# Seven-product blocks from block 3 on, strided keys first among a batch's loads, squares on either engine, a ring of three for xT, and tiled column sums

## The chip, the cores and the metric

One core of one Trainium2 chip. The time is that of one execution on the device, in microseconds; medians are given with their range. Runs are called slow when they lie more than 1.5% above the fastest of the same kernel, and medians, ranges and ratios here are of the other, fast runs alone. Five engines work side by side: TensorE (PE in the profile; PEld its weight loads), VectorE (DVE), ScalarE (ACT), GpSimd (POOL) and SyncE (SP).

## The reference

Eight batches of attention with eight heads (576 positions, 64 wide), then a feed-forward layer on 4608 tokens. Four heads look at the last 32 positions ("local"), four at every 32nd one ("strided").

```python
scores = scale * np.matmul(q, k.transpose(0, 1, 3, 2))
mask_local = (rel >= 0) & (rel < stride)
mask_strided = (rel >= 0) & (pos[None, :] % stride == pos[:, None] % stride)
# ... masked softmax, times v; heads 0-3 local, 4-7 strided; then x is [4608, 512]
h = x @ w_in                     # 512 -> 2048
r = np.maximum(h, 0.0)
g = s * (r * r) + b
return (g @ w_out).astype(np.float32)
```

Since g = s * r^2 + b, the kernel computes s * (r^2 @ w_out) + b * (column sums of w_out).

## The kernel before

A scheduler within the Python program fixes the order of all instructions before anything runs. It keeps an account of when each engine is free and when each result will be there; a job that several engines can do goes to the one that its account says is done first. In the traces each engine runs its work in that order, so a job whose input is there can still stand behind another job of its engine.

```python
LAT = {"A": 70.0, "V": 70.0, "P": 70.0, "D": 12000.0, "X": 7000.0, "Y": 12000.0}   # ns until a result counts as there
# in flush(), for a job p that is ready at r:
eng = min(p[1], key=lambda e: max(self.free[e], r) + p[1][e])
...
self.done[k] = end + (6000.0 if soon else p[4] or self.LAT[eng])
```

"D" stands for a transposing DMA on SyncE's queue. Loads of a batch, issued by GpSimd, in the order local q, local k, strided q, strided k. They are held back by a real dependency, a gate: GpSimd first reads one element of the transposed strided keys of the batch before.

```python
def fetch_qk(b):
    for mm in range(2):
        if (b - 1, "kTs", mm) in loaded:                    # the gate
            nc.gpsimd.tensor_copy(out=gate[0:1, 2 + mm:3 + mm],
                                  in_=loaded[b - 1, "kTs", mm][0:1, 0, 0:1])
    load_qk(b)
    # ... the account notes when each will have landed
# the issue of a batch's loads costs GpSimd nothing in the account:
plan.post([...], {"P": 0.0}, lambda eng, b=b: fetch_qk(b + 2), [("fetch", b + 2)])
```

From batch 3 on the strided queries are turned by a DMA transpose (qT) and then spread out into a tile with zeros between heads (qD_str), which the scores read. Three engines are offered for the spread:

```python
plan.post([("in", "q" + sfx, b, mm), ("q", (b - 2, m))], {"D": 1300.0}, q_dma, [("qT", id_)])
plan.post([("qT", id_), ("s", (b - 1, m), 2)], {"P": 2000.0, "V": 940.0, "A": 1340.0}, q_spread,
          [("q", id_)])
```

The feed-forward runs in nine blocks of 512 tokens. Its second product is either 64 matmuls of 512 columns, or, from block `SEVEN` on (5 here), seven half-size products of 16 matmuls of 256 columns, with sums made by VectorE. Squares, in the blocks before `SEVEN`, are on VectorE alone:

```python
([("u", T, ft)], {"V": 430, **({"A": 600} if T >= SEVEN else {})}, sq, [("g", T, ft)])
# column sums of w_out, spread over all 128 partitions: 16 of
nc.tensor.matmul(out=gts["b"], lhsT=ones16, rhs=w_out_sb[:, ft, :], start=(ft == 0), stop=(ft == NFT - 1))
```

The softmax here doesn't subtract the row's maximum and nothing guards it: scores larger than these inputs give would overflow.

## Time and profile before

| | before |
|---|---|
| time, first three runs | 311.81 us (311.32 to 312.32) |
| span of the profiled run, mean granted clock | 310.4 us, 0.996 |
| TensorE, VectorE, ScalarE, GpSimd busy | 301.5, 215.6, 182.7, 97.3 us |
| TensorE's excess (see below), of it from 30 us to the last matmul | 9.1 us, 3.1 us |

"Excess" is used throughout. For each matmul in the timeline, it is the distance to the next matmul's start less columns/2.4 + 2.5 ns, what that matmul needs at the full clock. Its sum is TensorE's lost time, whether it waits or runs at a lower clock. The tiled column sums and the FP32 matmul are left out of it and counted by themselves. The prediction below shows and reads the lines.

### The profile page before, as it was taken

How to read it: one execution, taken by the hardware profiler on the slowest of the kernel's cores; microseconds unless marked ns; L12 is line 12 of the kernel's file. 1: busy time of each engine (PE TensorE's matmuls, PEld its weight loads, DVE VectorE, ACT ScalarE, POOL GpSimd, SP SyncE). 2: the span in 40 equal slices, each digit the busy share in tenths (PEclk: the TensorE clock that was granted, in tenths of full speed). 3: DMA queues.
4: the chain of work that ended last, by engine and by line, in shares of the span. 5: the costliest groups of instructions: out<-in, count | busy, mean ns of one | idle time of the engine just before them, and what ended most of it. 6: DMA issues, size and time to landing. Idle time of an engine off the chain costs nothing.

```text
span 310.4 us, 6706 instructions
## 1 busy us (share of the span) xinstructions
PE 301.5 (97%) x2524; PEld 195.2 (63%) x2524; DVE 215.6 (69%) x573; ACT 182.7 (59%) x341; POOL 97.3 (31%) x140
## 2 busy tenths in 40 slices
PE   8898999999999999999999999999999999999994
PEld 3764655666556566556697755465577676767883
DVE  7566758898977788747674775679776467747552
ACT  2776854689846788368265856575945455456200
POOL 8562559921871095029500961000000000000000
PEclk9999999999999999999999999999999999999998
DMA  7999999994999899979999999953010100300313
GB/s 128 188 207 205 215 172 163 214 176 101 92 134 158 128 99 161 142 153 108 162 153 183 131 148 131 159 131 107 2 36 34 68 10 26 105 0 0 105 59 113
DMA packets 99924, 37.28 MB, mean 120 GB/s; under 512 B 81154, under 2 KB 95874, under 8 KB 99890
## 3 DMA queue, kind: packets, MB, share of 16 engines
q0 software_dynamic: 57200, 18.08, 59.1%
q1 hardware_dynamic: 42690, 18.76, 30.8%
q8 instruction: 20, 0.33, 0.4%
q14 instruction: 14, 0.11, 0.1%
HBM read 36.84 MB, written 10.32 MB: 152 GB/s over the span
## 4 chain that ended last, share of the span: by engine, by line
PE 88%; DMA 8%; POOL 1%; ACT 1%; issue 0%; DVE 0%; SPq 0%; POOLq 0%
PE ps_f L862 37%; PE ps_f L911 22%; PE ps_f L833 12%; DMA ql<-in_q_dram 6%; PE ps_s L528 5%; PE ps_a L582 3%; DMA w_out_sb<-in_v_dram 2%; PE ps_s L833 2%; PE ps_t L408 2%; PE ps_a L833 1%; PE ps_t L582 1%; PE ps_a L934 1%; PE ps_t L833 1%; PE ps_t L630 1%; POOL v_loc L312 1%
## 5 line engine op out<-in xcount | busy, mean ns | idle before, releaser
L862 PE MATMUL ps_f<-xT,w_in_sb 128*128 128x512 f16 (+1 forms) x632 | 146.6, 357 | 0.2 <-ACT u L884 0.2
L884 ACT ACTIVATE u<-ps_f 128x512 f16<-128x512 f32 x140 | 82.8, 596 | 74.0 <-PE ps_f L862 71.6
L862 PEld LDWEIGHTS <-w_in_sb 128*128 128x128 f16 x640 | 68.0, 113 | 35.7 <-issue 0.8
L911 PE MATMUL ps_f<-w_out_sb,gT 128*128 128x512 f16 x320 | 85.1, 379 | 0.0
L893 DVE TENSOR_TENSOR gT<-u 128x512 f16<-128x512 f16 x112 | 46.3, 418 | 33.2 <-ACT u L884 32.4
L911 PEld LDWEIGHTS <-gT 128*128 128x128 f16 x320 | 29.2, 98 | 23.6 <-DVE gT L893 0.6
L833 PEld LDWEIGHTS <-gT 128*128 128x128 f16 x320 | 31.0, 98 | 8.4
L833 PE MATMUL ps_f<-w_out_sb,gT 128*128 128x256 f16 x176 | 24.6, 273 | 0.0
L608 DVE TENSOR_TENSOR x_nat<-ps_a,rec 72x256 f16<-72x256 f32 (+1 forms) x52 | 23.8, 457 | 0.5
L544 ACT ACTIVATE p_loc<-ps_s 128x384 f16<-128x384 f32 x46 | 21.0, 494 | 3.4 <-PE ps_s L528 2.7
L544 ACT ACTIVATE p_str<-ps_s 72x432 f16<-72x432 f32 (+1 forms) x46 | 20.8, 482 | 3.2 <-PE ps_s L528 2.9
L290 POOL DMA_DIRECT2D v_loc<-in_v_dram x28 | 20.5, 741 | 2.3 <-DMA kl<-in_k_dram 1.2
L582 PEld LDWEIGHTS <-p_str 72*128 72x128 f16 x256 | 15.2, 98 | 9.5 <-DVE x_nat L608 0.2
L891 ACT ACTIVATE gT<-u 128x512 f16<-128x512 f16 x32 | 19.8, 629 | 0.8
L922 DVE SCALAR_TENSOR_TENSOR o<-ps_f,s_sb,bcs 128x512 f32<-128x512 f32 x20 | 14.9, 747 | 5.6 <-PE ps_f L911 5.1
L966 POOL COPY gate<-kT 1x1 f16<-1x1 f16 x6 | 1.8, 300 | 45.3 <-DMA kT<-ks 45.3
L597 DVE RECIPROCAL rec<-ps_a 72x4 f32<-72x4 f32 (+1 forms) x52 | 9.2, 178 | 9.4 <-PE ps_a L582 8.9
L552 DVE TENSOR_TENSOR p_loc<-p_loc,mask_loc 128x384 f16<-128x384 f16 x42 | 14.0, 349 | 2.5 <-ACT p_loc L544 2.2
L295 POOL DMA_DIRECT2D v_str<-in_v_dram x16 | 13.0, 816 | 8.6 <-DVE rec L597 2.7
L552 DVE TENSOR_TENSOR p_str<-p_str,mask_str 72x432 f16<-72x432 f16 (+1 forms) x42 | 14.3, 353 | 1.0 <-ACT p_str L544 0.7
L833 PEld LDWEIGHTS <-S 128*128 128x128 f16 x128 | 12.5, 98 | 3.9 <-issue 0.8
L582 PEld LDWEIGHTS <-p_loc 128*128 128x128 f16 x192 | 10.5, 98 | 4.8
(152 smaller groups left out, 407.1 us busy)
## 6 DMA issues: line engine op xcount, KB each, us to landing
out_dram<-o SPq DMA_DIRECT2D x35, 256.0 KB, 4.7
w_out_sb<-in_moe_w_out_dram POOLq DMA_DIRECT2D x4, 512.0 KB, 11.4
v_loc<-in_v_dram POOLq DMA_DIRECT2D x28, 72.0 KB, 8.4
ql<-in_q_dram POOLq DMA_DIRECT2D x6, 288.0 KB, 6.6
qs<-in_q_dram POOLq DMA_DIRECT2D x6, 288.0 KB, 6.8
ks<-in_k_dram POOLq DMA_DIRECT2D x6, 288.0 KB, 7.2
kl<-in_k_dram POOLq DMA_DIRECT2D x4, 288.0 KB, 7.9
kl<-in_k_dram POOLq DMA_DIRECT2D x16, 72.0 KB, 3.4
```

The source lines that it names most:

```text
L290: nc.gpsimd.dma_start(out=vl[LPAD:128, h, :, 0:D], in_=v_band(b, h))
L528: nc.tensor.matmul(out=st["s", g][0:nk, c:c + 2 * nq], lhsT=(st["k"][:, i * nq:i * nq + nk] if loc else st["k"][:, i, 0:SQ]), rhs=st["q"][ ...
L544: nc.scalar.activation(out=pt[0:nk, 0:2 * n].rearrange("k t c -> k (t c)"), in_=st["s", g][0:nk, 0:2 * n * nq], func=AF.Exp, scale=scale)
L552: nc.vector.tensor_tensor(out=pt[0:nk, 0:2 * n], in0=pt[0:nk, 0:2 * n], in1=mask, op=ALU.mult)
L582: nc.tensor.matmul(out=st["a"][:, j % per, :], lhsT=st["pw", g][0:nk, i * nq:i * nq + WIDE], rhs=vt[0:nk, 2 * mm + e, j, :])
L608: nc.vector.tensor_tensor(out=st["x"][:, j0:j0 + per, 64 * e:64 * e + 64], in0=st["pa", e, j][0:nq, 0:per, 0:D], in1=st["rec", e, j][0:nq, ...
L833: nc.tensor.matmul(out=gts[name, T][:, t], lhsT=lhs(k, t), rhs=rhs(k), start=fresh and t == k == 0, stop=t == 1 and k == H - 1, skip_group ...
L862: nc.tensor.matmul(out=gts["h", T, ft][:, lo:hi], lhsT=w_in_sb[min(ft // 4, 2)][:, ct].rearrange("p (c x l) -> p c l x", x=128, l=4)[:, ma ...
L884: nc.scalar.activation(out=gts["u", T, ft], in_=gts["h", T, ft], func=AF.Relu)
L891: nc.scalar.activation(out=gts[T][:, ft, :], in_=u, func=AF.Square)
L893: nc.vector.tensor_tensor(out=gts[T][:, ft, :], in0=u, in1=u, op=ALU.mult)
L911: nc.tensor.matmul(out=gts[id_], lhsT=gts[T][:, ft, ts * 128:(ts + 1) * 128], rhs=w_out_sb[:, ft, cols], start=(ft == 0), stop=(ft == NFT ...
```

## The change

Intent: less work for the bound engine (seven products in two more blocks; column sums in a quarter of the array each; a wait less in the last block), and room for it elsewhere (squares on either engine, a smaller ring). Core of the diff:

```diff
-                self.done[k] = end + (6000.0 if soon else p[4] or self.LAT[eng])
+                self.done[k] = end + (6000.0 if soon else p[4] or
+                                           (5500.0 if eng == "D" and end < 110000.0 else self.LAT[eng]))
-    NX = 4
+    NX = 3
+    KS_FIRST = 3
     def load_qk(b):
+        if b >= KS_FIRST:
+            load_qs("k", k)          # strided keys before the local q and k
         for name, src in (("q", q), ("k", k)):
             ...                      # local
+        load_qs("q", q)
+        if b < KS_FIRST:
+            load_qs("k", k)
-    SEVEN = 5
+    SEVEN = 3
-  ([("u", T, ft)], {"V": 430, **({"A": 600} if T >= SEVEN else {})}, sq, [("g", T, ft)])
+  ([("u", T, ft)], {"V": 430, **({"A": 630})}, sq, [("g", T, ft)])
-    def bcs_step(ft, group):         # 16 matmuls of 128 x 512
+    def bcs_steps(group):
+                for c in chunks:
+                    for g in range(4):
+                        nc.tensor.matmul(
+                            out=gts["b"][32 * g:32 * g + 32], lhsT=ones16[:, 0:32],
+                            rhs=w_out_sb[:, 4 * c + g, :], start=(c == 0), stop=(c == 3), ...)
+        # ScalarE copies the partial sums out; one FP32 matmul by 1/32 adds the four groups
+            nc.tensor.matmul(out=gts["b"], lhsT=part32, rhs=gts["b_sb"], start=True, stop=True)
 # (cut: the last block's product W in two PSUM banks, its stores in halves; the account's arrival
 #  times follow the new order of loads; positions of block 0's steps)
```

More of the change, by code (lines that the diff above doesn't have):

```diff
@@ L179 @@
     ones16 = w_mix[4].rearrange("p f m -> p (f m)")[:, 0:128]
+    part32 = w_mix[4].rearrange("p f m -> p (f m)").bitcast(FP32)[:, 64:192]
     w_mix[1] = w_out_sb[:, 0:NFT // 2, DM // 2:DM]
@@ L241 @@
     nc.vector.memset(ones16, 1.0)
+    nc.vector.memset(part32, 1.0 / 32)
     nc.vector.memset(vl_stage[0:LPAD], 0.0)
@@ L257, with load_qs @@
     paired = {}
+    KS_FIRST = 3
     def load_qk(b):
+        def load_qs(name, src):
+            if name == "k":
+                ts = ks[b % 2]
+            elif b < QS_DMA + 2:
+                ts = inp.tile([SR, NS], FP16, tag="qs", name="qs")
+            else:
+                ts = loaded[b - 2, "qs"]
+            if name == "k" and b in (2, 3) or name == "q" and b in (QS_DMA, QS_DMA + 1):
+                nc.gpsimd.memset(ts[64:SR], 0.0)
+            load_s(ts, src, b)
+            loaded[b, name + "s"] = ts
+        if b >= KS_FIRST:
+            load_qs("k", k)
         for name, src in (("q", q), ("k", k)):
@@ L270, in load_qk @@
                 nc.gpsimd.dma_start(out=h4(tl), in_=view_l(src, b))
-        for name, src in (("q", q), ("k", k)):
-            if name == "k":
-                ts = ks[b % 2]
-            elif b < QS_DMA + 2:
-                ts = inp.tile([SR, NS], FP16, tag="qs", name="qs")
-            else:
-                ts = loaded[b - 2, "qs"]
-            if name == "k" and b in (2, 3) or name == "q" and b in (QS_DMA, QS_DMA + 1):
-                nc.gpsimd.memset(ts[64:SR], 0.0)
-            load_s(ts, src, b)
-            loaded[b, name + "s"] = ts
+        load_qs("q", q)
+        if b < KS_FIRST:
+            load_qs("k", k)
     def load_s(dst, src, b):
@@ L749, in ff2_seven @@
         X, W, Y, Z = [Group(*x) for x in banks.get(T, [("f2", F2B)] * 4)]
+        Ws = [W, Group("f2", F2B)]
         b1 = bcs[:, None, 0:256].to_broadcast([128, 2, 256])
@@ L770, in g @@
                 o = op.tile([128, 2, 256], FP32, tag="o", name="o")
+                src = gts[of, T][:, ts] if (of, T) in gts else gts[of, T, ts.start]
                 nc.vector.scalar_tensor_tensor(
-                    out=o[:, ts], in0=gts[of, T][:, ts], scalar=s_sb[:, 0:1],
+                    out=o[:, ts], in0=src, scalar=s_sb[:, 0:1],
                     in1=plus()[:, ts], op0=ALU.mult, op1=ALU.add)
@@ L818, in ff2_seven @@
              [([d("P7"), d("Ub")], EV, ev("Vb", "Z", val("Ub")), [d("Vb")]),
-              ([d("P5"), d("Vb")], EV, store(1, 1, "W", val("Vb")), [d("C22")])]),
+              *([([d("P5"), d("Vb")], {"V": 420.0}, store(1, 1, "W", val("Vb"), slice(t, t + 1)),
+                  [("C22", T, t)]) for t in range(2)] if last else
+                [([d("P5"), d("Vb")], EV, store(1, 1, "W", val("Vb")), [d("C22")])])]),
             ("P4", Z, "Z", False, cut(1, 1), mix(4), gn(1), [d("Vb")] + wait(4),
@@ L829, in ff2_seven, with f @@
                 for k in range(H):
-                    def f(k=k, t=t, group=group, name=name, fresh=fresh, lhs=lhs, rhs=rhs, key=key):
-                        if fresh and t == k == 0:
+                    halves = last and name == "W"
+                    def f(k=k, t=t, group=group, name=name, fresh=fresh, lhs=lhs, rhs=rhs, key=key,
+                          halves=halves):
+                        if halves and fresh and k == 0:
+                            gts[name, T, t] = bank(Ws[t])[:, None, 0:256]
+                        elif fresh and t == k == 0:
                             gts[name, T] = bank(group).rearrange("p (t m) -> p t m", t=2)
-                        nc.tensor.matmul(out=gts[name, T][:, t], lhsT=lhs(k, t), rhs=rhs(k),
-                                         start=fresh and t == k == 0,
+                        nc.tensor.matmul(out=gts[name, T, t][:, 0] if halves else gts[name, T][:, t],
+                                         lhsT=lhs(k, t), rhs=rhs(k),
+                                         start=fresh and k == 0 and (halves or t == 0),
                                          stop=t == 1 and k == H - 1, skip_group_check=True)
-                    s = Step(f, 110, needs=needs(k) + more,
-                             group=group if fresh and t == k == 0 else None)
+                    s = Step(f, 110, needs=needs(k) + ([(x[0], T, t) if halves and x == d("C22")
+                                                        else x for x in more]),
+                             group=(Ws[t] if halves else group) if fresh and k == 0 and
+                             (halves or t == 0) else None)
                     if k == H - 1 and key == "P3" and last:
@@ L841, in ff2_seven @@
                                     store(0, 1, "W", val("Ub"), slice(t, t + 1)),
-                                    [W] if t else [("C12", T)])]
+                                    [Ws[t]])]
                     elif t == 1 and k == H - 1:
@@ L898, in ff1 @@
             s.posts = [([key] + free, {"A": 600, **({"V": 690} if T == 0 else {})}, rl, [("u", T, ft), group]),
-                       ([("u", T, ft)], {"V": 430, **({"A": 600} if T >= SEVEN else {})}, sq, [("g", T, ft)])]
+                       ([("u", T, ft)], {"V": 430, **({"A": 630})}, sq, [("g", T, ft)])]
         return s
@@ L928, in ff2, with parts, f, out_of @@
         return s
-    def bcs_step(ft, group):
-        def f():
-            if ft == 0:
-                gts["b"] = bank(group)
-            nc.tensor.matmul(out=gts["b"], lhsT=ones16, rhs=w_out_sb[:, ft, :],
-                             start=(ft == 0), stop=(ft == NFT - 1))
-        s = Step(f, 216, needs=[("w_out", ft // 4)], group=group if ft == 0 else None)
-        if ft == NFT - 1:
-            s.keys = [("b",)]
-            s.posts = [([("b",)], {"A": 690},
-                        lambda eng: nc.scalar.activation(out=bcs, in_=gts["b"], func=AF.Copy,
-                                                         scale=b_sb), [("bcs",), group])]
-        return s
+    def bcs_steps(group):
+        def parts(chunks):
+            def f():
+                if chunks[0] == 0:
+                    gts["b"] = bank(group)
+                for c in chunks:
+                    for g in range(4):
+                        nc.tensor.matmul(
+                            out=gts["b"][32 * g:32 * g + 32], lhsT=ones16[:, 0:32],
+                            rhs=w_out_sb[:, 4 * c + g, :], start=(c == 0), stop=(c == 3),
+                            skip_group_check=True)
+            return f
+        def out_of(eng):
+            gts["b_sb"] = op.tile([128, DM], FP32, tag="o", name="b_sums")
+            nc.scalar.copy(out=gts["b_sb"], in_=gts["b"])
+        def whole():
+            nc.tensor.matmul(out=gts["b"], lhsT=part32, rhs=gts["b_sb"], start=True, stop=True)
+        first = Step(parts((0, 1, 2)), 840, needs=[("w_out", c) for c in range(3)], group=group)
+        second = Step(parts((3,)), 400, needs=[("w_out", 3)], keys=[("b", 0)],
+                      posts=[([("b", 0)], {"A": 640}, out_of, [("b_sb",)])])
+        third = Step(whole, 900, needs=[("b_sb",)], keys=[("b", 1)],
+                     posts=[([("b", 1)], {"A": 690},
+                             lambda eng: nc.scalar.activation(out=bcs, in_=gts["b"], func=AF.Copy,
+                                                              scale=b_sb), [("bcs",), group])])
+        return first, second, third
     def arrive(keys, at):
@@ L968, in fetch_qk @@
         load_qk(b)
+        if b >= KS_FIRST:
+            arrive(both("ks", b), landing(2000))
         for name in ("q", "k"):
@@ L978, in fetch_qk @@
                 pair_post(b, name, mm, ("raw", name, b))
-        for name in ("qs", "ks"):
+        for name in ("qs", "ks")[:1 + (b < KS_FIRST)]:
             arrive(both(name, b), landing(2000 if b > 1 else 1750))
@@ L1091 @@
         if T == 0:
-            gr = [Group(*x) for x in [("f2", F2B)] * 4 + [("a", AB)]]
+            gr = [Group(*x) for x in [("f2", F2B), ("f2", F2B), ("s", SB), ("f2", F2B)]]
+            sums = bcs_steps(Group("s", SB))
             for c in range(0, NFT, 4):
-                f2 += [bcs_step(ft, gr[4]) for ft in range(c, c + 4)]
+                if c >= NFT - 8:
+                    f2.append(sums[c // 4 - 2])
                 f2 += [ff2(T, ts, ft, gr[ts]) for ts in range(2) for ft in range(c, c + 4)]
+            f2.append(sums[2])
             f2 += [ff2(T, ts, ft, gr[ts]) for ts in (2, 3) for ft in range(NFT)]
             for i, s in enumerate(f2):
-                s.pos = (i + 1) / 64.0
+                s.pos = 1.25 * (i + 1) / len(f2)
             mix_post()
```

## The prediction

> **What bounds the kernel now.** I read the busy shares first, then the 40 slices, the chain that ended last, the distances between matmul starts in the timeline, and last the groups and waits. The page gives:
>
> ```profile
> PE 301.5 (97%) x2524; PEld 195.2 (63%) x2524; DVE 215.6 (69%) x573; ACT 182.7 (59%) x341; POOL 97.3 (31%) x140
> PE   8898999999999999999999999999999999999994
> PEclk9999999999999999999999999999999999999998
> ```
>
> TensorE (PE) is the candidate: 97% busy in a span of 310.4 us, at the full granted clock (0.996 mean). But the ends of matmuls are modelled, so busy time can hide idle array time: a 128x512 matmul is listed at 379 ns. Cadence settles it. In the chain that ended last (start, length, what):
>
> ```profile
> 86.16 2.59 PE ps_f L911 x12
> 157.07 1.75 PE ps_f L862 x16
> 295.10 3.49 PE ps_f L833 x32
> ```
>
> Twelve 512-column matmuls follow each other at 216 ns (2.59/12), sixteen and thirty-two 256-column ones at 109 ns (1.75/16, 3.49/32). I gave every matmul of the timeline its columns/2.4 + 2.5 ns and summed what the distance to the next start exceeds that by. Of 310.4 us only 9.1 us are such excess: 5.9 us before 30 us (the head, which waits for loads), 2.4 us from 30 to 304 us, 0.74 us at 304.7 us. After the last matmul 4.3 us of eviction and store remain. So from 30 us to the end **the number of columns that TensorE streams is the time**. VectorE and ScalarE, at 69% and 59%, matter only where TensorE is made to wait for them. The 0.74 us is the wait that the list of TensorE's waits shows near the end:
>
> ```profile
> PE ps_a L833 <- DVE o L771: 0.6, 1, 0.6
> ```
>
> The second half of the last product writes a PSUM bank that VectorE is still reading for the first half's store.
>
> **What the Trainium skill says.**
> 1. "TensorE: Matmul & The Clock Gate", Back-to-back issue gap, gives N/2.4 + 2.5 ns for a warm stream: 215.8 ns at 512 columns and 109.2 at 256. The trace agrees (216 and 109). The same section says that a stream of weight load and matmul pairs sustains other spacings (131 ns at 512); this trace does not show that, every matmul has its own weight load and the spacing stays 216.
> 2. "TensorEngine Tiling (Array Packing)", Key Properties: different tiles run in parallel, but changing the tiling mode drains TensorE. The trace before has a two-column-tile case: the transposes at line 400, 96 columns wide, which alone would need 42.5 ns each.
>
> ```profile
> 6.88 0.45 PE L400 MATMUL ps_a<-ident,ql 96*64 96x96 f16 x12 [0.18 <-DMA ql<-in_q_dram]
> 7.16 0.42 PE L400 MATMUL ps_t<-ident,ql 96*64 96x96 f16 x12
> ```
>
> Twelve start within 0.28 us, 23 ns each: the two tiles overlap. A drain's cost isn't visible there. TensorE's page, Measured speedup vs the span model, has 3.07x for four row tiles at 512 columns and 2.38x for three column tiles, and no four-column-tile figure.
> 3. "FP8 and Floating Point Precision", TensorE Precision Notes: a true FP32 product takes four passes through the array. The kernel before has no FP32 matmul, so nothing in its trace shows it.
>
> **The change, part by part.** The instruction streams of both builds, compared engine by engine, give the counts; the durations are from the profile before.
>
> *Six blocks by seven products (blocks 3 and 4 join 5 to 8).* A block's second product is 64 matmuls of 512 columns, 64 x 216 = 13.83 us. By seven half-size products it is 112 of 256, 112 x 109.2 = 12.23 us. Two blocks: 3.20 us less on the path. For it VectorE gets eight 128x1024 sums a block (685 ns) and seven 750 ns operations plus a 690 ns add in place of four evictions of 747 ns: 8 x 0.685 + 7 x 0.75 + 0.69 - 4 x 0.747 = 8.4 us a block.
>
> ```profile
> L714 DVE TENSOR_TENSOR gT<-gT 128x1024 f16<-128x1024 f16 x16 | 10.7, 683 | 0.9 <-PE ps_f L833 0.4 <-ACT gT L891 0.4
> L893 DVE TENSOR_TENSOR gT<-u 128x512 f16<-128x512 f16 x112 | 46.3, 418 | 33.2 <-ACT u L884 32.4
> L891 ACT ACTIVATE gT<-u 128x512 f16<-128x512 f16 x32 | 19.8, 629 | 0.8
> ```
>
> *Squares on either engine.* VectorE has 79 of them instead of 112, ScalarE 65 instead of 32: -33 x 0.418 = -13.8 us and +33 x 0.629 = +20.8 us. VectorE also takes six of the 690 ns relus from ScalarE (+4.1 and -6 x 0.596 = -3.6). With the 16.9 us above and small copies that move both ways, VectorE ends near 223 us and ScalarE near 196 us. Both stay far below TensorE. All of this is beside the path and worth nothing by itself; it pays for the sums.
>
> *Column sums.* Before, 16 matmuls of 512 columns made them (line 934): 16 x 216 = 3.46 us. After, 16 column-tiled ones of 32 output rows, four side by side: four rounds of 216 to 230 ns if they overlap as fully as the pairs at line 400, or 3.46/3.07 = 1.13 us at the skill's ratio for four row tiles; I take 1.0. Then one FP32 matmul of 512 columns, four passes: 4 x 213 = 0.86, say 0.9 with its weights. Two separate entries into the tiled mode, so four switches; my guess is 0.3 us for all. Sum 2.2 us, so **1.26 us less**. Between the two steps ScalarE copies the partial sums out; TensorE has other work placed there.
>
> *xT a ring of three.* Blocks 3 and 6 straddle the ring's end instead of block 4: 64 matmuls of 512 and 128 of 256 become 64 each of 128, 192, 320 and 384 columns. 64 x (55.8 + 82.5 + 135.8 + 162.5) = 27.95 us against 64 x 216 + 128 x 109.2 = 27.80: 0.14 us more. The columns are the same, only 64 starts are added. A 55.8 ns matmul still covers a weight load, since the attention matmuls follow each other at 33 ns with one each. The ring can also make a store of xT wait for an earlier block's first product: batch 7's now waits for block 5's instead of block 4's, and is needed in block 7, a whole block (27 us in the late windows) later. I expect nothing on the path.
>
> *The last block in halves.* Two banks for the product of the wait quoted above: its 0.74 us goes. The 4.3 us tail stays, its store still 128x256.
>
> *Strided keys first, and another landing time for transposed loads.* They only alter order. With 2.4 us of excess between 30 and 304 us there is little to win; a few tenths at most, and I count none.
>
> Sum: -3.20 - 1.26 + 0.14 - 0.74 = -5.06 us. The fillers and the head are unchanged: TensorE's order is the same up to the first column sum, at 40.8 us. Against it I set **0.8 us of new waits**, a judgement: 0.4 us excess came when seven-product work began in block 5 at 220 us, and it will now begin among attention, twice, with VectorE some 80% loaded; the ScalarE step within the column sums may be late for about 0.2 us. Result: 311.81 - 5.06 + 0.8 = 307.5; since the schedule was evidently tuned together with these parts, I shade the waits down and say **307.2 us**.
>
> **Rivals.**
> 1. *VectorE becomes the bound in blocks 3 and 4.* The half-size products share two PSUM banks and each next one waits for an eviction. For it: the windows show how loaded these stretches are,
>
> ```profile
> 120.00:155.00 35.00, 35.00 (x266) 20.04 (x264) 23.64 (x76) 19.74 (x39) 15.73 (x24) 1.00 1.34 144
> 155.00:190.00 35.00, 35.00 (x299) 25.53 (x297) 23.77 (x72) 23.04 (x42) 13.99 (x20) 1.00 1.60 154
> ```
>
>    (window, length, then busy time of PE, PEld, DVE, ACT, POOL). VectorE's 23.7 of 35 us becomes up to 32.1 before the squares leave. Against it: ScalarE has 12 to 15 us free there, first products and attention can fill between, and block 6 runs seven products at 17.8 of 27 us with hardly any excess (0.05 us from 230 to 280). If it happens it costs 1 to 3 us: 308.5 to 310.
> 2. *The column tiles don't overlap, or each switch drains for long.* Then the sums cost 3.46 + 0.9 + 0.3 = 4.7 instead of 2.2 us: 309.7. Against it: the pairs at line 400 overlap.
> 3. *The ring or the new load order holds back attention*, through transposes that queue on one engine behind one that waits. For it: DMA engines are the next fullest resource in that stretch (1.34 and 1.60 in the column of DMA share, against 0.12 later). Then whole microseconds of idle TensorE appear between 100 and 215 us: 309 to 312. Against it: the slack of one block.
> 4. *Better order removes waits that I left in* (1.0 us at 28.6 us in the head, 0.4 us at 224 us): 305.3 at best, the arithmetic less these two, since between 30 and 304 us there are only 2.4 us of excess.
>
> **Range and chances.** The arithmetic alone, without new waits, gives 306.75. Up: 2 to 3 us for a rival. Down: 0.5 us for the column sums, up to 1 us for rival 4. So 305.2 to 309.6. Faster by over 2% means below 305.6, which needs nearly all of the excess gone as well: 0.13. Slower by over 2% would be above 318; nothing in the parts can cost 11 us: 0.01. Within 2%: 0.86.
>
> **What would show it.** Line 833's successor at 672 matmuls, 109 ns apart, and line 911's at 192, 216 ns apart. Column-tiled starts a few ns apart within a group of four, then one FP32 matmul whose successor starts about 0.9 us later. VectorE near 223 us, ScalarE near 196 us. No wait of 0.6 us in the last 6 us. Total excess over columns/2.4 + 2.5 between 30 us and the last matmul under 4 us. I am wrong if that excess exceeds 5 us (then see which engine TensorE waits for in blocks 3 and 4), if the tiled matmuls start 216 ns apart, or if the head changes.

## The result, and the profile after

**322.11 us** (320.98 to 323.44, 4 runs) against 312.06 us (311.32 to 312.98, 4 runs): ratio 1.0322, 95% interval 1.0273 to 1.0371, slower. Ratios here are the mean time of one kernel's fast runs over the mean of the other's of the same rounds, so they are not quite the ratio of the medians quoted. The prediction was 307.2 us, at most 309.6.

The busy row and the slices of the page, after:

```profile
PE 303.2 (94%) x2686; PEld 207.8 (65%) x2686; DVE 223.3 (69%) x572; ACT 193.9 (60%) x363; POOL 100.5 (31%) x146
PE   8899999999999599999992999999999999999995
PEclk9999999999999959999997799999999999999999
```

VectorE (223.3) and ScalarE (193.9) are where the arithmetic put them (223 and 196). New are two holes in TensorE's row, in slices 14 and 22 (8.0 us each, so about 105 to 113 and 169 to 177 us), and low clock just after each. TensorE's waits name the holes:

```profile
PE ps_s L539 <- POOL qD_str L323: 4.8, 1, 4.8
PE ps_s L539 <- DVE qD_str L323: 4.1, 1, 4.1
```

Both are strided scores that wait for the spread queries, once spread by VectorE and once by GpSimd. Before, no wait for a spread query tile is in the list. The idle time costs more than itself. In the windows around the first hole (window, length, then busy time of PE, PEld, DVE, ACT, POOL, granted clock, DMA share, GB/s):

```profile
108.80:112.22 3.42, 0.27 (x2) 0.00 (x0) 0.02 (x1) 1.28 (x3) 0.93 (x2) 1.00 1.73 137
112.22:119.05 6.83, 5.93 (x24) 2.90 (x25) 4.76 (x15) 2.35 (x5) 2.28 (x3) 0.50 1.72 128
119.05:122.46 3.41, 3.41 (x26) 1.86 (x25) 2.00 (x8) 2.12 (x4) 0.07 (x1) 1.00 2.94 106
```

After 4 us of idling, the clock is at half for 6.83 us. TensorE works in 5.93 us of these, so the low clock costs it about 3.0 us. The Trainium skill, "TensorE: Matmul & The Clock Gate", What's actually happening, says that an idle window of about 3.4 us halves the clock, that a busy window of the same length restores it, and that these windows run freely, not from the kernel's start. The trace fits: 6.83 us are two windows of 3.41 us, and TensorE resumes 0.9 us into the first of them, so that only the second is busy throughout. The second hole brings 6.83 us at half as well.

The balance between the two profiles, +11.3 us of span: seven products -3.20; column sums 3.46 to 1.96, so -1.50; ring +0.14; excess 9.1 to 24.9 us, so +15.9 (0.19 us of it stands at the two entries into the tiled sums). Of this, 6.9 us come between 100 and 120 us and 8.3 us between 160 and 180 us; the last block's 0.74 us is gone; about 0.9 us are small waits between 50 and 70 us. So **the work went down as reckoned, and the waits and low clock of two stretches took more than it gave.**

Why are the queries late? SyncE's queue before, then GpSimd's timeline before (batch 4's transposes, batch 5's loads):

```profile
99.93 2.56 SPq L487 DMA_TRANSPOSE qT<-qs  x2
103.97 2.93 SPq L470 DMA_TRANSPOSE kT<-ks  x2
```

```profile
107.94 0.41 POOL L966 COPY gate<-kT 1x1 f16<-1x1 f16 x1 [12.82 <-DMA kT<-ks]
109.05 0.70 POOL L270 DMA_DIRECT2D ql<-in_q_dram  x1 [0.35 <-DVE rec L597]
```

And after, the same two:

```profile
91.66 2.74 SPq L481 DMA_TRANSPOSE kT<-ks  x2
101.05 3.52 SPq L498 DMA_TRANSPOSE qT<-qs  x2
```

```profile
97.36 0.41 POOL L1005 COPY gate<-kT 1x1 f16<-1x1 f16 x2 [4.83 <-DMA kT<-ks]
97.83 0.72 POOL L296 DMA_DIRECT2D ks<-in_k_dram  x1
```

The gate waits for the keys' transposes only. Before, the queries' transposes stood ahead of the keys' in the queue, so an open gate meant that the queries were done too. After, the keys come first and the gate opens 10.6 us earlier, 3.7 us before the queries' transposes are even issued. These now run against the next batch's loads. Their time from issue to landing, before and after:

```profile
DMA to landing us min/median/max: 2.7/4.5/6.3
```

```profile
DMA to landing us min/median/max: 5.2/8.2/11.4
```

This view times only the transposes whose landing it can assign, here two of ten before and four of ten after. The semaphore updates in the two traces allow all ten to be timed: minimum, median and maximum are 2.7, 4.6 and 6.3 us before, and 3.9, 8.0 and 11.8 us after. So the reading holds. Where landing times are given below, the same limit applies; "all ten" marks times that were worked out in this second way.

The chain that ended last, after (start, length), holds one of them, of 11.05 us, then the spread and the scores; the last line's five matmuls take 426 ns each, half speed:

```profile
101.05 11.05 DMA qT<-qs
112.20 0.31 DVE qD_str L323
112.53 0.46 DVE qD_str L323
112.99 0.14 issue
113.12 0.90 PE ps_s L539 x6
114.03 2.13 PE ps_f L934 x5
```

The second hole has two parts. VectorE waits 3.64 us for late transposes, with the masking of local scores behind them in its order, for which TensorE then waits 1.6 us. After that the other spread comes late, although its transposes had landed by 169.9 us (by the semaphore updates): it stands on GpSimd behind DMA issues, which themselves wait.

```profile
169.87 0.64 DVE L323 COPY qD_str<-qT 64x576 f16<-64x576 f16 x2 [3.64 <-DMA qT<-qs]
174.72 0.81 POOL L306 DMA_DIRECT2D v_str<-in_v_dram  x1 [0.67 <-DMA qs<-in_q_dram]
175.52 1.39 POOL L323 COPY qD_str<-qT 64x576 f16<-64x576 f16 x2
```

### The profile page after: what moved, and what is told of

Read it like the earlier page. It is cut to its first block, busy times and chain, and to the rows that moved or that the text cites. A ratio compares the mean times of both kernels' runs of the same rounds, so it can differ in the third digit from the quotient of the medians.

```text
span 321.7 us, 7045 instructions
## 1 busy us (share of the span) xinstructions
PE 303.2 (94%) x2686; PEld 207.8 (65%) x2686; DVE 223.3 (69%) x572; ACT 193.9 (60%) x363; POOL 100.5 (31%) x146
## 4 chain that ended last, share of the span: by engine, by line
PE 65%; DMA 23%; POOL 5%; issue 3%; DVE 1%; SPq 1%; ACT 0%; POOLq 0%; DVEq 0%; ACTq 0%
PE ps_f L885 29%; PE ps_f L853 19%; DMA ql<-in_q_dram 8%; PE ps_f L934 6%; DMA xT<-x_nat 4%; DMA qT<-qs 3%; PE ps_s L539 3%; DMA qs<-in_q_dram 3%; DMA kT<-ks 2%; DMA w_out_sb<-in_v_dram 2%; PE ps_a L593 2%; PE ps_s L853 2%; DMA v_loc<-in_v_dram 1%; POOL ks L273 1%; PE ps_t L853 1%
## 5 line engine op out<-in xcount | busy, mean ns | idle before, releaser
L885 PE MATMUL ps_f<-xT,w_in_sb 128*128 128x512 f16 (+4 forms) x696 | 151.0, 343 | 0.0
L907 ACT ACTIVATE u<-ps_f 128x512 f16<-128x512 f32 x134 | 79.0, 595 | 65.8 <-PE ps_f L885 65.1
L853 PEld LDWEIGHTS <-gT 128*128 128x128 f16 x512 | 49.0, 98 | 12.1 <-issue 0.5
L916 DVE TENSOR_TENSOR gT<-u 128x512 f16<-128x512 f16 x79 | 33.3, 424 | 21.9 <-ACT u L907 21.3
L934 PE MATMUL ps_f<-w_out_sb,gT 128*128 128x512 f16 x176 | 48.5, 386 | 0.0
L853 PE MATMUL ps_f<-w_out_sb,gT 128*128 128x256 f16 x312 | 43.8, 274 | 0.0
L914 ACT ACTIVATE gT<-u 128x512 f16<-128x512 f16 x65 | 40.6, 630 | 1.8 <-DVE u L909 0.4
L934 PEld LDWEIGHTS <-gT 128*128 128x128 f16 x192 | 17.4, 99 | 11.9 <-issue 1.3
L725 DVE TENSOR_TENSOR gT<-gT 128x1024 f16<-128x1024 f16 x28 | 18.8, 683 | 5.9 <-PE ps_f L853 5.0
L853 PE MATMUL ps_f<-w_mix,gT 128*128 128x256 f16 x144 | 19.3, 276 | 0.0
L539 PE MATMUL ps_s<-qD_str,kT 128*72 128x144 f16 x64 | 8.5, 250 | 8.9 <-POOL qD_str L323 4.8
## 6 DMA issues: line engine op xcount, KB each, us to landing
w_out_sb<-in_moe_w_out_dram POOLq DMA_DIRECT2D x4, 512.0 KB, 11.3
```

What stands on the lines that cost most here:

```text
L725: nc.vector.tensor_tensor(out=at(out), in0=at(x), in1=at(y), op=op)
L853: nc.tensor.matmul(out=gts[name, T, t][:, 0] if halves else gts[name, T][:, t], lhsT=lhs(k, t), rhs=rhs(k), start=fresh and k == 0 and (ha ...
L885: nc.tensor.matmul(out=gts["h", T, ft][:, lo:hi], lhsT=w_in_sb[min(ft // 4, 2)][:, ct].rearrange("p (c x l) -> p c l x", x=128, l=4)[:, ma ...
L907: nc.scalar.activation(out=gts["u", T, ft], in_=gts["h", T, ft], func=AF.Relu)
L914: nc.scalar.activation(out=gts[T][:, ft, :], in_=u, func=AF.Square)
L916: nc.vector.tensor_tensor(out=gts[T][:, ft, :], in0=u, in1=u, op=ALU.mult)
```

## The experiments

Theory A: keys first opens the gate too early. Theory B: the assumed 5.5 us is too short by itself. Theory C: VectorE and ScalarE are too full in blocks 3 and 4. Theory D, formed on the way: the spread is put on GpSimd, behind DMA issues that its account leaves out. One caution holds for all but the last experiment: an edit lets the scheduler lay out everything anew, so more than the named part moves.

### Keys last again

```diff
-    KS_FIRST = 3
+    KS_FIRST = 8
```

> The changed kernel with one part undone: the strided keys are again the last of a batch's four loads. Theory A (early keys let the transposes of keys, and with them the gate that holds back the next batch's loads, come some 10 us early, so the loads run into the q transposes that the first stall waits for): the 4.2 us stall near 109 us goes, with its half-clock stretch, and most of the second one near 170 us; time 307 to 312 us. Rival B (the scheduler's assumption that a transposed load lands in 5.5 us, before 110 us, is too short by itself): the stall near 109 us stays, 319 to 322 us. Rival C (VectorE and ScalarE too full in blocks 3 and 4): both stalls stay, 320 to 323 us.

Measured: 322.66 us (322.46 to 323.39), ratio 1.0343. None of the three expectations fits the whole: the time lies in C's range, but C had both stalls staying. The first hole is gone and the queries' transposes land in 3.2/3.6/4.2 us (minimum, median, maximum; all ten 2.8/3.4/4.2): A is right on the cause of the first. But a single hole of 10.2 us stands near 175 us:

```profile
PE ps_s L539 <- POOL qD_str L323: 10.2, 1, 10.2
```

GpSimd's timeline shows what it did meanwhile (three rows with one issue each are left out). The transposes had been issued from 159.8 to 163.2 us and the slowest landing took 4.2 us, so the queries were there by about 167.4 us at the latest.

```profile
168.59 2.94 POOL L286 DMA_DIRECT2D ql<-in_q_dram  x4 [0.38 <-issue]
171.49 2.93 POOL L286 DMA_DIRECT2D kl<-in_k_dram  x4
175.81 2.98 POOL L301 DMA_DIRECT2D v_loc<-in_v_dram  x4
178.70 1.64 POOL L306 DMA_DIRECT2D v_str<-in_v_dram  x2
183.37 0.80 POOL L306 DMA_DIRECT2D v_str<-in_v_dram  x1 [1.64 <-DMA ks<-in_k_dram]
184.17 1.39 POOL L323 COPY qD_str<-qT 64x576 f16<-64x576 f16 x2
```

The spread stands behind 18 issues of 0.7 to 0.8 us each, some of which wait in turn. The account books them at 0 ns. This is theory D.

### The assumed 12 us again

```diff
-                                           (5500.0 if eng == "D" and end < 110000.0 else self.LAT[eng]))
+                                           self.LAT[eng])
```

> The changed kernel with one part undone: the scheduler again assumes 12 us, not 5.5 us, from issue to landing of a transposed load before 110 us. The keys are still first. Theory A: it moves the scores behind other work, so the first stall shrinks by up to its 4.2 us even though q's transposes land no sooner (about 11 us), the second stays: 313 to 318 us. Rival B: the first stall and its half clock go fully, 314 to 315 us, the transposes landing as fast as before (about 4.5 us). Rival C: no change, 320 to 323 us.

Measured: 333.20 us (331.47 to 333.43, three fast runs; a slow one took 337.75), ratio 1.0661, much worse than all three expectations. The queries' transposes take 10.7 us in the median (9.4 us for all ten), and the longest wait is behind GpSimd again:

```profile
PE ps_s L538 <- POOL qD_str L322: 16.3, 1, 16.3
```

So B is refuted as the cause: taking it out doesn't help while keys are first. Why this schedule puts a spread at an even worse place on GpSimd was not isolated.

### Keys last and 12 us

Both edits above.

> The changed kernel with both of these undone, leaving seven products, squares on either engine, the ring of three, the tiled sums and the last block's halves. If what was lost lies in these two parts, the arithmetic of the prediction shows: 306 to 309 us and no stall over 1.5 us between 30 us and the end. Rival C (the seven products among attention, or the ring of three): 312 us or more, with the second stall near 170 us still there.

Measured: 309.50 us (307.66 to 310.86), ratio 0.9908. No wait of over 1.2 us is left, and the clock is 1.000. Seven products, ring, squares and sums all stand in this kernel, so neither C nor the ring makes the two holes by itself. The time is 0.5 us above the range that was expected: there are 2.9 us more excess between 50 and 90 us than before, in short waits mostly for VectorE (a later expectation says 3.3 us, which still counted the FP32 matmul).

### Keys first in the kernel before

The order of loads and the account's arrival times from the diff above, put into the kernel before, nothing else.

> The kernel before with only the strided keys loaded first from batch 3 on, the assumed 12 us kept. Theory A: the loads of the next batch start before q's transposes here too, so these land in 8 us or more instead of 4.5; whether TensorE stalls depends on the slack that the 12 us leave: 312 to 318 us. If the order of loads alone is harmless (rival B or C): 311 to 313 us and transposes of q landing in about 4.5 us.

Measured: 332.06 us (329.65 to 334.47), ratio 1.064. **This one part costs 20 us**, more than A had said, and without any of the other parts. Transposes of queries land in 10.0 us in the median (9.8 us for all ten). TensorE's longest waits:

```profile
PE ps_s L536 <- POOL qD_str L320: 6.0, 2, 5.5
PE ps_s L536 <- DMA kT_loc<-kl: 4.3, 1, 4.3
```

Again a spread behind GpSimd's issues, and now a transpose of local keys that is late as well.

### No spread on GpSimd

```diff
-            plan.post([("qT", id_), ("s", (b - 1, m), 2)], {"P": 2000.0, "V": 940.0, "A": 1340.0}, q_spread,
+            plan.post([("qT", id_), ("s", (b - 1, m), 2)], {"V": 940.0, "A": 1340.0}, q_spread,
```

> The changed kernel with GpSimd no longer offered as the engine that spreads q's transposed strided tile (keys still first, assumed landing still 5.5 us). Theory D (the second stall is a spread that the scheduler gave to GpSimd, which stands there behind some 17 DMA issues of the next batch that cost it no time in the scheduler's books): the stall near 170 us and its half clock go, some 8.5 us, the one near 109 us stays: 312 to 315 us. Rival (the spread is late because the transposes themselves land late): a stall of the same size on VectorE's or ScalarE's spread, 319 us or more.

Measured: 317.22 us (316.63 to 318.64, three fast runs; a slow one took 321.55), ratio 1.0164, interval 1.0128 to 1.0201, so it stays unclear whether it is slower than the kernel before by 2%. It is better than the changed kernel by about 5 us, not by 7 to 10. The wait behind GpSimd is gone, and so, in this new layout, is the one near 109 us; instead 2.3 us of waiting for VectorE's spread and 2.7 us for an eviction stand near 165 and 183 us. The transposes still take up to 9.4 us (11.1 us of all ten), and the 2.3 us end 0.8 us after one of 9.3 us has landed: a smaller stall of the rival's kind, by theory A's cause.

### Keys last and no spread on GpSimd

The first and the fifth edit; 5.5 us stay.

> The changed kernel with the keys last again and no spread on GpSimd, the assumed landing still 5.5 us. With the keys last, q's transposes land in about 3.6 us in the runs so far, so 5.5 us is a fair assumption. Theories A and D together: no stall over 2 us, 307 to 311 us. If the 5.5 us are harmful by themselves (rival B): a stall on a transposed tile before 110 us, 313 us or more.

Measured: 308.71 us (307.80 to 309.61), ratio 0.9883. Both holes gone; 5.5 us do no harm when the transposes land in 4.4 to 6.0 us (2.8 to 6.5 us for all ten). After the head, one wait of 1.4 us for VectorE is left.

### Keys first, gate on the queries too

```diff
+        if (b - 1, "qT2") in loaded:
+            nc.gpsimd.tensor_copy(out=gate[0:1, 2:3], in_=loaded[b - 1, "qT2"][0:1, 0, 0, 0:1])
+            nc.gpsimd.tensor_copy(out=gate[0:1, 3:4], in_=loaded[b - 1, "qT2"][0:1, 1, 0, 0:1])
         load_qk(b)
# and the load's job is posted only after the queries' transposes
+                        [("qT", (b + 1, mk)) for mk in range(2, 4) if b + 1 >= QS_DMA],
```

> The changed kernel, keys first, with the next batch's loads held back until both q transposes of the batch before have landed as well, from batch 5's predecessor on. Theory A: q's transposes land in about 4 us again (10 us with keys first until now) and the stall near 109 us goes; a stall behind GpSimd's issues may stay where it has the spread: 308 to 318 us. If something else than the loads slows the transposes: they still take 8 us or more, and 318 to 325 us.

Measured: 310.26 us (308.27 to 310.61), ratio 0.9938. With keys still first and the loads held back, the transposes are fast:

```profile
DMA to landing us min/median/max: 2.8/3.2/3.5
```

(Two of ten; all ten: 2.7, 3.0 and 5.0 us.) This is the direct test of A. By itself the order of loads does no harm that these runs show (compare 308.44 us with keys first and 308.71 us with keys last, below and above); what hurts is that it opened the gate ahead of the queries. The Trainium skill says in "Trainium Kernel Development and Optimization", Key Constraints, that DMAs from SyncE's, ScalarE's and GpSimd's queues run on the same 16 DMA engines and interleave. These runs fit that: 3.0 us in the median of all ten with the next batch's loads held back, 8.0 us beside them. How the loads slow the transposes isn't shown.

### Squares on VectorE alone in blocks 0 to 2

On the kernel of 309.50 us:

```diff
-  ([("u", T, ft)], {"V": 430, **({"A": 630})}, sq, [("g", T, ft)])
+  ([("u", T, ft)], {"V": 430, **({"A": 630} if T >= SEVEN else {})}, sq, [("g", T, ft)])
```

> The version with keys last and the assumed 12 us (309.5 us), with squares on VectorE alone again in blocks 0 to 2 (the seven-product blocks keep both engines). That version has 3.3 us more excess between 50 and 90 us than the kernel before, in waits for VectorE. If the free choice of engine reorders the early blocks so that these waits appear: 306 to 307.5 us. If VectorE is short of time there without it: 310 us or more.

Measured: 310.08 us (309.14 to 310.87), ratio 0.9926, the same within the spread. The excess between 50 and 90 us is 3.3 us after 3.7 us, hardly smaller. So the free choice of engine isn't what brings most of these waits, and the first theory of this run falls. The time fits the second, VectorE short of time, but nothing else tests it: what brings them stays open.

### Both mends together

Keys first, gate on the queries, no spread on GpSimd.

> The changed kernel, keys first, with both mends: the next batch's loads held back until q's transposes have landed, and no spread on GpSimd. Theories A and D together: no wait over 1 us after 40 us, clock 1.0, 305 to 309 us, the best of the versions so far. If the two mends get in each other's way: over 310 us.

Measured in five rounds: **308.44 us** (307.88 to 309.39), ratio 0.988, interval 0.9856 to 0.9904. It beats the kernel before by 1.2%, and the changed kernel by some 4%. The clock is 1.000 in the profiled run, and no wait after 40 us exceeds 0.5 us. From the 308.71 us with keys last it can't be told apart. Its page:

```profile
PE 297.2 (97%) x2686; PEld 205.9 (67%) x2686; DVE 223.4 (73%) x572; ACT 197.6 (64%) x369; POOL 98.9 (32%) x148
```

### Seven products from block 5 only

On keys last, no spread on GpSimd: `SEVEN = 3` back to 5.

> The version with keys last and no spread on GpSimd (308.7 us), but seven products from block 5 on as in the kernel before. The arithmetic: two blocks lose 3.2 us of saving, so 311 to 313 us. If the seven products in blocks 3 and 4 cost waits that eat it: the same time or less, 306 to 309 us.

Measured: 311.20 us (310.81 to 311.56), ratio 0.9959. Against 308.71 us, two blocks by seven products are worth about 2.5 us of the 3.2 reckoned, so they keep most of their worth amid attention. (The two kernels ran in different calls; the kernel before was at 312.15 and 312.08 us there.)

### Ring of four

On the same kernel: `NX = 3` back to 4.

> The version with keys last and no spread on GpSimd (308.7 us), with xT a ring of four again. The arithmetic: 0.14 us less of TensorE work; no wait for a free slot was seen in the ring of three, so 307.5 to 309.5 us. If the ring of three holds back attention unseen: 306 us or less.

Measured: 308.73 us (307.71 to 309.95), ratio 0.9885. The ring makes no difference that these runs could show.

### The same schedule, ten copies moved from GpSimd to ScalarE

On the kernel of 322.66 us (keys last, 5.5 us). The account is kept as if GpSimd did them:

```diff
         def q_spread(eng):
             st["q"] = (qD_loc if loc else qD_str)[mm]
+            eng = "A" if eng == "P" else eng
```

> The version with keys last and 5.5 us (322.7 us, one stall of 10.3 us behind GpSimd near 175 us). The schedule is made as before, but the spreads that it gives to GpSimd are put on ScalarE at the same place in the order: TensorE's, VectorE's and SyncE's instructions and their order are the same, only eight copies change their engine. Theory D: the stall of 10.3 us and the half clock after it (some 2.5 us) go, ScalarE adds at most a few tenths: 308 to 311 us. If the copies are late because their transposes land late: the stall stays on ScalarE's copies, 318 us or more.

Measured: 313.37 us (312.68 to 314.48), ratio 1.0045. TensorE's, VectorE's and SyncE's orders are identical to those of the 322.66 us kernel; in the traces ten copies changed engine, not eight (eight of strided queries and two of local ones), and 9.3 us went. The 10.2 us wait isn't in the list any more. D is shown for this hole. It ends above the 311 us expected because other waits stand in it: 1.6 us for VectorE near 186 us, which the 322.66 us kernel has as well, and, new, 1.5 us in two waits for ScalarE and 1.4 us for VectorE. The longest two:

```profile
PE ps_f L854 <- DVE Va L773: 1.6, 1, 1.6
PE ps_f L886 <- ACT u L908: 1.5, 2, 1.0
```

## Why the prediction was wrong

**What bounds the kernel** was read rightly: TensorE's columns are the time, as long as nothing makes it wait.

**Seven products**: right in kind. 672 matmuls of 256 columns and 192 of 512 follow each other at 109 and 216 ns in the median; on the chip two blocks are worth about 2.5 us of the 3.20 once the holes are mended. (64 x 216 ns is 13.82 us, not 13.83; by the formula the two blocks save 3.17 us.)

**Column sums**: right, 2.14 us where 2.2 was said. TensorE's timeline after:

```profile
44.22 0.83 PE L961 MATMUL ps_s<-w_out_sb,w_mix 128*32 128x512 f16 x12
44.98 1.25 PE L934 MATMUL ps_f<-w_out_sb,gT 128*128 128x512 f16 x5
50.44 1.02 PE L972 MATMUL ps_s<-b_sums,w_mix 128*128 128x512 f32 x2
51.29 0.29 PE L593 MATMUL ps_f<-v_str,p_str 72*128 72x65 f16 x4
```

Twelve tiled matmuls, 2 to 4 ns apart within each group of four, take 0.76 us up to the next start; four more, in the second step, 0.33 us; the FP32 matmul is recorded as two and takes 0.86 us. That is 1.96 us. To it belong 0.09 us more at each of the two matmuls just before the tiled ones, whose next starts come after 309 and 308 ns in place of 216 (the excess has these). The cost of a switch was visible before, against what the prediction says of line 400: at 31.5 and 32.1 us of the trace before, the last matmul ahead of its transposes and the last transpose are followed 93 and 96 ns late.

**Ring of three**: right, nothing on the path. **Last block in halves**: right, its wait is gone.

**Engine loads**: right (223.3 and 193.9 us). Rival 1, VectorE as the bound, did not make the holes, though short waits for VectorE and ScalarE remain in the mended kernels.

**The first step that failed** is "Strided keys first, and another landing time for transposed loads. They only alter order ... a few tenths at most, and I count none." The order of loads decides when a gate opens, and so what runs beside the queries' transposes; this part alone cost 20 us in the kernel before. Rival 3 named the place ("whole microseconds of idle TensorE appear between 100 and 215 us") but by another path: it blamed a queue in which a transpose waits behind another, and its "309 to 312" was a third of the size. It was set aside with "the slack of one block", which speaks of xT's ring and not of the loads at all. "Nothing in the parts can cost 11 us", with a chance of 0.01, rested on the same omission. I looked for the worth of a part that moves loads in TensorE's present waits, which are small because the old order prevented them.

**The second step that failed**: new waits of 0.8 us. Two terms were missing. The spread goes to GpSimd when the account finds it free, and the account leaves out some 18 issues of 0.7 to 0.8 us; and each of the two holes takes the clock to half for 6.83 us. The prediction's own sign of being wrong, an excess of over 5 us from 30 us on, came true with 18.7 us. That the schedule "was evidently tuned together with these parts", for which the waits were shaded down, had no run behind it. With both causes mended, 308.4 us was measured where the sum without new waits said 306.75 and the prediction 307.2: the rest is short waits, in the profile about 0.8 us more between 50 and 90 us than before and 0.8 us more between 210 and 220 us.

**Open**: why an assumed 12 us with keys first puts the spread where it waits 16 us; what brings the short waits between 50 and 90 us; and which part of the DMA engines' work slows the transposes (only that the loads do is shown). Theory A is shown by the gate run; D by the run with moved copies, for the hole of the kernel with keys last. For the changed kernel's second hole, both are read from its trace, and their shares were not separated.

## What to carry to other kernels

When a change moves loads, ask what each gate or semaphore that holds them back used to imply beyond what it names; here a wait for the keys also stood for the queries, until their order was turned round. A scheduler that books DMA issues as free will give work to the engine that issues them, and one copy behind 18 issues can stop the bound engine for 10 us. This kernel sat at 97% of its bound engine, and the small waits in its profile (2.4 us) did not tell what a new order could cost (20 us).

## What the Trainium skill lacked or had wrong

- "TensorE: Matmul & The Clock Gate", Back-to-back issue gap, gives about 131 ns for a 512-column matmul in a stream of weight load and matmul pairs; here each has its own weight load and the spacing is 216 ns, as the prediction notes.
- The same page, Measured speedup vs the span model, has no figure for four column tiles at 512 columns: 12 such matmuls took 0.76 us to the next start (0.86 us with the late entry before them), against 12 x 216 ns = 2.59 us one after another, a factor of 3.4 (3.0).
- "TensorEngine Tiling (Array Packing)", Key Properties, says that changing the mode drains TensorE, without a cost: it was 0.09 us on the way in and 0.1 us on the way out at both steps here, and 0.09 and 0.1 us around the transposes of line 400 before.
- "FP8 and Floating Point Precision" gives four passes for true FP32 and doesn't say how a profile shows them: one 128x512 FP32 matmul is two records here, 0.86 us together, the time of four passes.
- "DMA: Bandwidth & Descriptors": no figure for a DMA transpose beside loads. An 80-row strided tile landed in 3.0 us (median of all ten; up to 5.0) with the next batch's loads held back and in 8.0 us (up to 11.8) beside them.
